# Attention products over 64 rows in pairs, and the float64 decode moved from attention to the experts

## Chip, core and metric

The kernel runs on one core of one Trainium2 chip. The metric is device time in microseconds (us) of one execution. Engines are TensorE (PE, with its weight loads listed as PEld), VectorE (DVE), ScalarE (ACT), GpSimd (POOL) and SyncE (SP), which issues transfers.

## The reference, cut to what matters

```
scores = (z @ z.T) / 3072            # 8 batches, 3072 x 64 each
x = u * (max(scores, 0)**2 @ v)      # v, u: 3072 x 256
e = argmax(x @ w_gate)               # 24576 tokens, 8 experts
x = gate * eom * (max(x @ w1[e], 0) @ w2[e])     # 256 -> 1024 -> 256
h = x @ w_in                         # w_in, w_out: float64
out = (h * sigmoid(h)) @ w_out       # 256 -> 2048 -> 256
```

All data but w_in and w_out are float32.

## The kernel before

There are three stages, one after the other. Every large product is made of rounded float32 numbers ("fp32r"): a float is split into a rounded part `hi` and a rest `lo`, and a product is the sum of hi*lo, lo*hi and hi*hi. `split` makes the two: the rounded copy on VectorE or ACT (L106, L108), the rest on VectorE (L109).

**Attention.** A chunk is 512 query columns; there are 48 chunks (6 for each of 8 batches), and each runs over 24 steps of 128 keys, 1152 steps in all. A step is `s_step` (scores, 2 products of 512 columns), `act_r` (relu on ACT), `act_a` (square on ACT), `dve_hl` (hi and lo on VectorE) and `v_step` (6 products of 512 columns that add up in two PSUM banks over the whole chunk, one for each half of v's 256 columns). As z has only 64 rows, `s_step` stacks z's hi and lo as one stationary tile `st` of 128 rows, made by `z_prep2` through two transfers on SP's queue, and multiplies it by z's hi and then z's lo, each of which stands twice, one below the other.

Program order is an order written out by hand: scores run 3 steps ahead of the sums (LOOK), and two tables of tasks (`pe_tasks` ahead of the step's sums, `tasks` behind) place the rest: loads, splits of v and z, the finished chunk's product with u (`x_mul`), its gate products (`gate_mm` at step 5, 4 products of 512 columns), `rank_mm` (step 10, 5 small products), page bookkeeping, `rep_mm` (step 14, 4 small ones) and the scatters of rows to `x_d` by POOL. [...]

`w_last` decodes the float64 weights of the last stage in 32 jobs of 256 columns: a load, 12 VectorE operations and one ACT copy, and a store of hi and lo to `wio_d`. The jobs run in attention, spread over the steps of a chunk.

**Experts.** 103 tiles of 256 tokens with 4 iterations each (412). An iteration is `s1` (12 products of 256 columns), a relu on ACT and a rest on VectorE, and `v1` (12 products of 256 columns), which runs two iterations behind `s1`. `w_split` splits the gathered weights (copy on ACT, rest on VectorE) four to six iterations ahead; `x1_prep` transposes and splits the next tile's tokens. ACT's queue reloads the decoded weights from `wio_d` in eight transfers.

**Last stage.** 768 iterations of 12 products of 512 columns, not touched by the change.

Of the kernel before, what the change touches and what calls it, by code (L numbers as in the profile page):

```python
# [30 lines left out]
P = 128  # L31
# [13 lines left out]
LOOK = 3  # L45
NEARLY = 20
# [6 lines left out]
def fused_kernel(ctx: ExitStack, tc: tile.TileContext, uT, v, zT, wg, w1, w2, w_in, w_out, out):  # L53
# [7 lines left out]
    wio_d = dram.tile([P, 2 * 2 * 2 * DFF], F32, name="wio_d")  # L61
# [3 lines left out]
    ps_s = ctx.enter_context(tc.tile_pool(name="ps_s", bufs=2, space=bass.MemoryType.PSUM))  # L65
    ps_a = ctx.enter_context(tc.tile_pool(name="ps_a", bufs=4, space=bass.MemoryType.PSUM))
    ps_m = ctx.enter_context(tc.tile_pool(name="ps_m", bufs=2, space=bass.MemoryType.PSUM))
# [110 lines left out]
    HH, LL, ST, ZZ, VH, VL, VR, UT = {}, {}, {}, {}, {}, {}, {}, {}  # L178
# [7 lines left out]
    def z_prep1(b, c):  # L186
        hh = zp.tile([P, CH], F32R, name="hh", tag="hh", bufs=6)
        ll = zp.tile([P, CH], F32R, name="ll", tag="ll", bufs=6)
        split(hh, ll, ZZ.pop((b, c)), "v" if b == 0 and c < 2 else "a")
        HH[b, c], LL[b, c] = hh, ll  # L190

    def z_prep2(b, c):
        st = zp.tile([P, CH], F32R, name="st", tag="st", bufs=9)
        if (b, c) == (0, 0):
            sc.activation(st[:DQK], HH[b, c][:DQK].bitcast(F32), AF.Copy)
            ve.tensor_copy(st[DQK:], LL[b, c][DQK:].bitcast(F32))
        else:
# [22 lines left out]
    wtmp = [small.tile([P, WJ], I32, name=f"wt{i}") for i in range(3)]  # L220
    NWJ = 2 * DFF // WJ

    def w_last(job):
        which, part = divmod(job, NWJ)
        src = (w_in, w_out)[which]
        raw = small.tile([P, WJ], I64, name="wraw", tag="wraw", bufs=1)
        sy.dma_start(raw, src[:, part * WJ:(part + 1) * WJ])
        words = raw.bitcast(I32).rearrange("p (n w) -> p n w", w=2)
        lw, hw = words[:, :, 0], words[:, :, 1]
        hi = small.tile([P, WJ], F32R, name="whi", tag="whi", bufs=1)  # L230
        lo = small.tile([P, WJ], F32R, name="wlo", tag="wlo", bufs=1)
        t, m, r = wtmp
        tf, mf, rf = (x.bitcast(F32) for x in wtmp)

        def store():
# [395 lines left out]
    for k in range(LOOK):  # L631
# [5 lines left out]
        if k < LOOK - 1:  # L637
            act_a(k)
            dve_hl(k)
# [405 lines left out]
```

## Time and profile before

| | |
|---|---|
| median of 3 runs | 5479.15 us (5478.13 to 5480.53) |
| the profiled execution | 5476.75 us, its span 5475.0 us |
| TensorE busy | 5449.3 us |
| VectorE, ACT, POOL busy | 4481.3, 2866.0, 2071.7 us |
| granted TensorE clock | 0.999 of full speed, mean |

The span runs from the first to the last instruction of the profiled execution. Busy time of an engine is the union of its instructions; consecutive matmuls overlap in it, so the distance of their starts says more than the length of one. Attention runs to about 2175 us, the experts to about 3380 us.

### The profile page before, as it was taken

To read this page: it belongs to the slowest core of one execution; us is meant where nothing else is said; L and a number is where in the kernel's file an instruction comes from. 1 tells how busy PE (TensorE), PEld (TensorE's weight loads), DVE (VectorE), ACT (ScalarE), POOL (GpSimd) and SP (SyncE) were. 2 spreads that over 40 slices of the span, in tenths; PEclk is the share of its full clock that TensorE was granted. 3 is DMA by queue.
4 is the path that set the end of the run, shared out by engine and by line. 5 is a ranking of instruction groups with operands and counts; after the bars stand their busy time and mean duration, and the time that the engine had idled before them with its cause. 6 is when DMAs were issued, how large, how long until landed. Compare 5 with 4: busy or idle time off the path is not lost.

```text
span 5475.0 us, 84633 instructions
## 1 busy us (share of the span) xinstructions
PE 5449.3 (100%) x28952; PEld 4690.0 (86%) x28952; DVE 4481.3 (82%) x9832; ACT 2866.0 (52%) x5076; POOL 2071.7 (38%) x1961
## 2 busy tenths in 40 slices
PE   9999999999999999999999999999999999999999
PEld 7888888888888887999999999888888888888887
DVE  8999999999999887878777777777777777777776
ACT  7777777777777766666666665222222222222222
POOL 0343333333333333443333335433333333333331
PEclk9999999999999999999999999999999999999999
DMA  8212121212122101244222221101000000100000
GB/s 281 63 54 63 51 62 51 62 53 60 55 58 55 50 24 53 80 146 164 93 78 78 78 78 37 26 24 28 24 24 25 24 24 24 28 24 24 25 24 21
DMA packets 160243, 314.99 MB, mean 58 GB/s; under 512 B 58560, under 2 KB 66752, under 8 KB 152384
## 3 DMA queue, kind: packets, MB, share of 16 engines
q0 software_dynamic: 95152, 156.97, 9.8%
q1 hardware_dynamic: 63504, 144.22, 8.3%
q10 hardware_dynamic: 1152, 8.39, 0.4%
q8 instruction: 226, 3.70, 0.3%
q14 instruction: 209, 1.71, 0.1%
HBM read 346.83 MB, written 112.72 MB: 84 GB/s over the span
## 4 chain that ended last, share of the span: by engine, by line
PE 96%; DVE 2%; issue 1%; DMA 0%; ACT 0%; POOL 0%; POOLq 0%; SPq 0%; DVEq 0%; ACTq 0%
PE s L854 19%; PE s L741 11%; PE acc L762 11%; PE acc L297 9%; PE acc L298 9%; PE acc L299 9%; PE acc L878 6%; PE acc L877 6%; PE acc L876 6%; PE sc L269 4%; PE sc L270 4%; PE lg L325 1%; DVE lo L109 0%; DVE hi L108 0%; DVE vl L109 0%
## 5 line engine op out<-in xcount | busy, mean ns | idle before, releaser
L466 POOL DMA_INDIRECT x_d<-z,xi x768 | 803.7, 1046 | 1422.0 <-DVE lo L109 812.2
L810 POOL DMA_INDIRECT yg<-y_d,yi x768 | 810.9, 1056 | 1216.0 <-DVE l L109 1106.1
L861 ACT ACTIVATE sg<-s 128x512 f32<-128x512 f32 x768 | 459.3, 598 | 1524.6 <-PE s L854 1342.0
L854 PE MATMUL s<-yh,wi 128*128 128x512 f32 x3072 | 1070.4, 389 | 0.1
L275 ACT ACTIVATE r<-sc 128x512 f32<-128x512 f32 x1152 | 688.6, 598 | 537.2 <-PE sc L270 512.5
L297 PE MATMUL acc<-hi,vl 128*128 128x512 f32 x2304 | 906.9, 394 | 0.0
L298 PE MATMUL acc<-lo,vh 128*128 128x512 f32 x2304 | 899.8, 391 | 1.4 <-DVE lo L109 1.4
L299 PE MATMUL acc<-hi,vh 128*128 128x512 f32 x2304 | 897.4, 389 | 0.0
L862 DVE TENSOR_TENSOR sg<-s,sg 128x512 f32<-128x512 f32 x768 | 531.2, 692 | 417.6 <-ACT sg L861 393.6
L109 DVE TENSOR_TENSOR lo<-a,hi 128x512 fp32r<-128x512 f32 x1152 | 798.9, 693 | 39.6
L280 ACT ACTIVATE a<-r 128x512 f32<-128x512 f32 x1152 | 726.4, 631 | 99.1 <-DVE lo L109 70.9
L854 PEld LDWEIGHTS s<-yh,wi 128*128 128x128 f32 x3072 | 576.6, 188 | 120.2 <-issue 0.5
L741 PE MATMUL s<-x1h,w0b 128*128 128x256 f32 x3296 | 662.9, 284 | 9.8 <-DVE w0b L109 9.7
L762 PE MATMUL acc<-w1b,h 128*128 128x256 f32 x3296 | 660.7, 283 | 0.0
L854 PE MATMUL s<-yl,wi 128*128 128x512 f32 x1536 | 597.7, 389 | 0.5 <-issue 0.5
L878 PE MATMUL acc<-h,wo 128*128 128x512 f32 x1536 | 597.5, 389 | 0.0
L877 PE MATMUL acc<-l,wo 128*128 128x512 f32 x1536 | 597.5, 389 | 0.0
L876 PE MATMUL acc<-h,wo 128*128 128x512 f32 x1536 | 597.5, 389 | 0.0
L108 DVE CAST hi<-a 128x512 fp32r<-128x512 f32 x1152 | 497.2, 432 | 87.4 <-ACT a L280 69.4
L741 PEld LDWEIGHTS s<-x1h,w0b 128*128 128x128 f32 x3296 | 545.0, 192 | 11.0 <-DVE w0b L109 9.3
L109 DVE TENSOR_TENSOR l<-sg,h 128x512 fp32r<-128x512 f32 x768 | 531.9, 693 | 26.5
L762 PEld LDWEIGHTS acc<-w1b,h 128*128 128x128 f32 x3296 | 543.7, 192 | 0.1
(200 smaller groups left out, 9655.0 us busy)
## 6 DMA issues: line engine op xcount, KB each, us to landing
x_d<-zero SPq DMA_DIRECT2D x25, 1024.0 KB
vr<-in_v_dram SPq DMA_DIRECT2D x48, 512.0 KB
ut<-in_uT_dram SPq DMA_DIRECT2D x48, 512.0 KB
out_dram<-ot SPq DMA_DIRECT2D x48, 512.0 KB
zz<-in_zT_dram SPq DMA_DIRECT2D x96, 128.0 KB
x_d<-z,xi POOLq DMA_INDIRECT x768
yg<-y_d,yi POOLq DMA_INDIRECT x768
st<-hh SPq DMA_DIRECT2D x47, 128.0 KB
```

The costliest lines, as they stand in the source:

```text
L109: return ve.tensor_sub(lo, src, hi.bitcast(F32))
L297: pe.matmul(ACC[q][dc], vl[:, j % 4, ds_], hi, start=(j == 0), stop=False)
L298: pe.matmul(ACC[q][dc], vh[:, j % 4, ds_], lo, start=False, stop=False)
L299: pe.matmul(ACC[q][dc], vh[:, j % 4, ds_], hi, start=False, stop=(j == NJ - 1))
L466: i = gp_.indirect_dma_start(x_u, bass.IndirectOffsetOnAxis(ap=xi4[:, q * NB + c:q * NB + c + 1], axis=0), Z[q][:, c, :], None, bounds_che ...
L741: pe.matmul(ps[:, i, :], wb[:, hl, dc, fs], xx[:, dc, :], start=(n == 0), stop=(n == 5))
L762: pe.matmul(acc[:, h, :], x[:, i, ts], wb[:, hl, i, :], start=first, stop=end, skip_group_check=True)
L810: i = gp_.indirect_dma_start(YG[m][:, c, :], None, y_u[:n, :], bass.IndirectOffsetOnAxis(ap=yi4[:, m * NB + c:m * NB + c + 1], axis=0), bo ...
L854: pe.matmul(ps, wi[:, hl, dc, fs], xx[:, dc, :], start=(n == 0), stop=(n == 5))
L876: pe.matmul(acc, wo[:, 1, fc, es], hi, start=(fc == 0), stop=False)
L877: pe.matmul(acc, wo[:, 0, fc, es], lo, start=False, stop=False)
L878: pe.matmul(acc, wo[:, 0, fc, es], hi, start=False, stop=(fc == FC2 - 1))
```

## The change

Scores are computed for two steps at once: `s_part` issues three products (hi*lo, lo*hi, hi*hi), each as two matmuls over 64 rows. The first uses rows 0 to 63 and belongs to the first step, the second uses rows 64 to 127 and belongs to the second step; they write two different banks. `v_part` issues each of the sums' products as two matmuls over 64 rows, too, each half with a PSUM bank of its own, so a chunk has four banks of sums. At the chunk's end `x_sum` copies one half from PSUM on ACT and adds the other on VectorE. The stationary tile `st` and its transfers are gone. Scores share four banks with the small products. Scores run six steps ahead. At four steps of a chunk the hi copy is made by ACT instead of VectorE. Some loads and splits of z are placed at other steps. The decode jobs run in the experts from iteration 96 on and write straight into the tiles that the last stage reads; `wio_d`, its stores and its reloads are gone, and the tables for the last stage are computed from iteration 73 on instead of 120. `x_gather` has three buffers instead of four, and the first `x1_prep` stands ahead of the fourth gather.

```diff
@@ -43,6 +43,9 @@
 HD = D // 4
 NFIRST = CH // T + E - 1
 LOOK = 3
+LA = 6
+ON_ACT = (7, 10, 11, 12)
+HP = P // 2
 NEARLY = 20
 QEARLY = NQ - 3
 WJ = 256
@@ -58,13 +61,11 @@
     dram = ctx.enter_context(tc.tile_pool(name="dram", bufs=1, space=bass.MemoryType.DRAM))
     x_d = dram.tile([NSLOT * P, 2 * T], F32, name="x_d")
     y_d = dram.tile([NSLOT * P, 2 * T], F32, name="y_d")
-    wio_d = dram.tile([P, 2 * 2 * 2 * DFF], F32, name="wio_d")
     x_u = x_d[:, :].rearrange("r (u c) -> (r u) c", c=HD)
     y_u = y_d[:, :].rearrange("r (u c) -> (r u) c", c=HD)
-    ps_s = ctx.enter_context(tc.tile_pool(name="ps_s", bufs=2, space=bass.MemoryType.PSUM))
+    ps_s = ctx.enter_context(tc.tile_pool(name="ps_s", bufs=4, space=bass.MemoryType.PSUM))
     ps_a = ctx.enter_context(tc.tile_pool(name="ps_a", bufs=4, space=bass.MemoryType.PSUM))
-    ps_m = ctx.enter_context(tc.tile_pool(name="ps_m", bufs=2, space=bass.MemoryType.PSUM))
     const = ctx.enter_context(tc.tile_pool(name="const", bufs=1))
     ident = const.tile([P, P], F32, name="ident")
@@ -184,20 +185,10 @@
         ZZ[b, c] = zz
     def z_prep1(b, c):
-        hh = zp.tile([P, CH], F32R, name="hh", tag="hh", bufs=6)
-        ll = zp.tile([P, CH], F32R, name="ll", tag="ll", bufs=6)
+        hh = zp.tile([P, CH], F32R, name="hh", tag="hh", bufs=9)
+        ll = zp.tile([P, CH], F32R, name="ll", tag="ll", bufs=9)
         split(hh, ll, ZZ.pop((b, c)), "v" if b == 0 and c < 2 else "a")
         HH[b, c], LL[b, c] = hh, ll
-
-    def z_prep2(b, c):
-        st = zp.tile([P, CH], F32R, name="st", tag="st", bufs=9)
-        if (b, c) == (0, 0):
-            sc.activation(st[:DQK], HH[b, c][:DQK].bitcast(F32), AF.Copy)
-            ve.tensor_copy(st[DQK:], LL[b, c][DQK:].bitcast(F32))
-        else:
-            sy.dma_start(st[:DQK].bitcast(F32), HH[b, c][:DQK].bitcast(F32))
-            sy.dma_start(st[DQK:].bitcast(F32), LL[b, c][DQK:].bitcast(F32))
-        ST[b, c] = st
     def v_load(b, g):
         vr = zp.tile([P, 4, D], F32, name="vr", tag="vr", bufs=2)
@@ -217,44 +208,6 @@
         UT[q] = ut
-    wtmp = [small.tile([P, WJ], I32, name=f"wt{i}") for i in range(3)]
-    NWJ = 2 * DFF // WJ
-
-    def w_last(job):
-        which, part = divmod(job, NWJ)
-        src = (w_in, w_out)[which]
-        raw = small.tile([P, WJ], I64, name="wraw", tag="wraw", bufs=1)
-        sy.dma_start(raw, src[:, part * WJ:(part + 1) * WJ])
-        words = raw.bitcast(I32).rearrange("p (n w) -> p n w", w=2)
-        lw, hw = words[:, :, 0], words[:, :, 1]
-        hi = small.tile([P, WJ], F32R, name="whi", tag="whi", bufs=1)
-        lo = small.tile([P, WJ], F32R, name="wlo", tag="wlo", bufs=1)
-        t, m, r = wtmp
-        tf, mf, rf = (x.bitcast(F32) for x in wtmp)
-
-        def store():
-            for h, x in ((0, hi), (1, lo)):
-                o = (which * 2 + h) * 2 * DFF + part * WJ
-                sy.dma_start(wio_d[:, o:o + WJ], x.bitcast(F32))
-
-        return [
-            lambda: ve.tensor_scalar(t, lw, 29, 7, ALU.logical_shift_right, ALU.bitwise_and),
...
-            store,
-        ]
-
-
     SC, RR, AA, HI, LO, ACC = {}, {}, {}, {}, {}, {}
     def bcj(k):
@@ -262,17 +215,34 @@
         b, c = divmod(q, NCH)
         return q, b, c, j
-    def s_step(k):
-        q, b, c, j = bcj(k)
-        ps = ps_s.tile([P, CH], F32, name="sc", tag="sc")
-        lhs = ST[b, j // 4][:, (j % 4) * P:(j % 4 + 1) * P]
-        pe.matmul(ps, lhs, HH[b, c], start=True, stop=False)
-        pe.matmul(ps, lhs, LL[b, c], start=False, stop=True)
-        SC[k] = ps
+
+
+    def halves(x, y, a, b, start, stop):
+        return [
+            pe.matmul(out, x[h][h * HP:(h + 1) * HP, w], y[h][h * HP:(h + 1) * HP, m], start=start, stop=stop,
+                      skip_group_check=True)
+            for h, (w, m, out) in enumerate((a, b))
+        ]
+
+    def s_part(k, parts):
+
+        for i in range(2):
+            if k + i not in SC:
+                SC[k + i] = ps_s.tile([P, CH], F32, name="sc", tag="sc")
+        at_ = []
+        for i in range(2):
+            q, b, c, j = bcj(k + i)
+            at_.append((b, c, j // 4, slice(j % 4 * P, (j % 4 + 1) * P), SC[k + i]))
+        for n in parts:
+            wx, mx = ((HH, LL), (LL, HH), (HH, HH))[n]
+            halves(
+                [wx[b, g] for b, c, g, js, ps in at_], [mx[b, c] for b, c, g, js, ps in at_],
+                *[(js, slice(0, CH), ps) for b, c, g, js, ps in at_], n == 0, n == 2,
+            )
     def act_r(k):
-        r = ap_.tile([P, CH], F32, name="r", tag="r", bufs=2)
-        sc.activation(r, SC.pop(k), AF.Relu, scale=1.0 / S)
+        r = ap_.tile([P, CH], F32, name="r", tag="r", bufs=3)
+        sc.activation(r, SC[k], AF.Relu, scale=1.0 / S)
         RR[k] = r
     def act_a(k):
@@ -281,32 +251,40 @@
         AA[k] = a
     def dve_hl(k):
-        hi = ap_.tile([P, CH], F32R, name="hi", tag="hi", bufs=4)
-        lo = ap_.tile([P, CH], F32R, name="lo", tag="lo", bufs=4)
-        beat.append(split(hi, lo, AA.pop(k)))
+        hi = ap_.tile([P, CH], F32R, name="hi", tag="hi", bufs=6)
+        lo = ap_.tile([P, CH], F32R, name="lo", tag="lo", bufs=6)
+        beat.append(split(hi, lo, AA.pop(k), "a" if k % NJ in ON_ACT else "v"))
         HI[k], LO[k] = hi, lo
-    def v_step(k):
+    def v_part(k, d):
+
         q, b, c, j = bcj(k)
-        if j == 0:
-            ACC[q] = [ps_a.tile([P, CH], F32, name=f"acc{d}", tag="acc") for d in range(2)]
-        hi, lo = HI.pop(k), LO.pop(k)
-        vh, vl = VH[b, j // 4], VL[b, j // 4]
-        for dc in range(2):
-            ds_ = slice(dc * P, (dc + 1) * P)
-            pe.matmul(ACC[q][dc], vl[:, j % 4, ds_], hi, start=(j == 0), stop=False)
-            pe.matmul(ACC[q][dc], vh[:, j % 4, ds_], lo, start=False, stop=False)
-            pe.matmul(ACC[q][dc], vh[:, j % 4, ds_], hi, start=False, stop=(j == NJ - 1))
+        if q not in ACC:
+            ACC[q] = [[ps_a.tile([P, CH], F32, name=f"acc{i}{h}", tag="acc") for h in range(2)] for i in range(2)]
+        hi, lo = HI[k], LO[k]
+        vh, vl = VH[b, j // 4][:, j % 4, :], VL[b, j // 4][:, j % 4, :]
+        ds_ = slice(d * P, (d + 1) * P)
+        for n, (v, x) in enumerate(((vl, hi), (vh, lo), (vh, hi))):
+            halves([v, v], [x, x], *[(ds_, slice(0, CH), ACC[q][d][h]) for h in range(2)],
+                   j == 0 and n == 0, j == NJ - 1 and n == 2)
     XH, XL, Z, G = {}, {}, {}, {}
-    def x_mul(q, dc):
+    def x_sum(q, dc):
         if dc == 0:
             XH[q] = xp.tile([P, 2, CH], F32R, name="xh", tag="xh", bufs=1)
             XL[q] = xp.tile([P, 2, CH], F32R, name="xl", tag="xl", bufs=1)
             Z[q] = xp.tile([P, NB, HD], F32, name="z", tag="z", bufs=3)
-        ve.tensor_mul(UT[q][:, dc, :], ACC[q][dc], UT[q][:, dc, :])
+        n = NB // 2
+        t = Z[q][:, dc * n:(dc + 1) * n, :].rearrange("p n c -> p (n c)")
+        sc.activation(t, ACC[q][dc][1], AF.Copy)
+        ve.tensor_add(t, ACC[q][dc][0], t)
+
+    def x_mul(q, dc):
+        n = NB // 2
+        t = Z[q][:, dc * n:(dc + 1) * n, :].rearrange("p n c -> p (n c)")
+        ve.tensor_mul(UT[q][:, dc, :], t, UT[q][:, dc, :])
     def x_hi(q, dc):
         sc.activation(XH[q][:, dc, :], UT[q][:, dc, :], AF.Copy)
@@ -318,7 +296,7 @@
         ve.transpose(Z[q][:, :, dc * Q:(dc + 1) * Q], UT[q][:, dc, :])
     def gate_mm(q):
-        ps = ps_m.tile([P, CH], F32, name="lg", tag="misc")
+        ps = ps_s.tile([P, CH], F32, name="lg", tag="sc")
         n = 0
         for dc in range(2):
             for xx in (XL[q], XH[q]):
...
@@ -567,9 +545,7 @@
         last = first + (NCH - 1) * NJ
         for c in range(NCH):
             at(first + c * NJ + 12, z_load, b, c)
-            at(first + c * NJ + 26, z_prep1, b, c)
-            at(first + c * NJ + 28 if c < 3 else last + 4 * (c - 3) + 4 if c < NCH - 1 else last + 28,
-               z_prep2, b, c)
+            at(first + c * NJ + 20 if c < 3 else last + (4, 8, 20)[c - 3], z_prep1, b, c)
             s1_ = first + (c + 1) * NJ + 16 if c < 3 else last + (6, 15, 17)[c - 3]
             at(s1_ - 6, v_load, b, c)
             at(s1_, v_prep, b, c, 0)
@@ -598,29 +574,21 @@
                 left.append((q, [c]))
     for s, f in ((13, order1), (16, order1_mm), (16, order2), (19, order2_mm), (19, order3)):
         at((QEARLY + 1) * NJ + s, f, 0, pe=f in ON_PE)
-    WSTEPS = (8, 9, 13, 15, 16, 17, 18, 19, 21, 21, 22, 22, 23, 23)
-    for job, q in zip(range(2 * NWJ), [q for q in range(1, NQ) if q % NCH < NCH - 1]):
-        k = q * NJ
-        at(k + 2, lambda k=k, job=job: [at(k + i, f) for i, f in zip(WSTEPS, w_last(job))])
-
     z_load(0, 0)
     v_load(0, 0)
     z_load(0, 1)
     z_prep1(0, 0)
-    z_prep2(0, 0)
     z_load(0, 2)
     v_load(0, 1)
     z_prep1(0, 1)
-    z_prep2(0, 1)
     at(0, v_load, 0, 2)
     at(0, z_prep1, 0, 2)
-    at(0, z_prep2, 0, 2)
     at(3, u_load, 0)
     at(3, lambda: sy.dma_start(wgr, wg))
     for c in range(3, NCH):
-        at(4 * c - 9, lambda c=c: (z_load(0, c), v_load(0, c)))
-        at(4 * c - 7, z_prep1, 0, c)
-        at(4 * c - 6, z_prep2, 0, c)
+        at(4 * c - 12, z_load, 0, c)
+        at(4 * c - 9, v_load, 0, c)
+        at(4 * c - 9, z_prep1, 0, c)
     for c in range(1, NCH):
         at(max(4 * c - 4, 0), v_prep, 0, c, 0)
         at(4 * c - 3, v_prep, 0, c, 1)
@@ -628,27 +596,38 @@
     for i in range(0, NSLOT, 4):
         at(5 + i if i < 12 else 11 + i // 2, zero_pages, i, 4)
     at(6, gate_matrix)
-    for k in range(LOOK):
-        s_step(k)
+    for k in range(LA):
+        if k % 2 == 0:
+            s_part(k, (0, 1, 2))
         act_r(k)
         if k == 0:
             v_prep(0, 0, 0)
             v_prep(0, 0, 1)
-        if k < LOOK - 1:
+        if k < LA - 2:
             act_a(k)
             dve_hl(k)
     for k in range(NSTEP):
-        if k + LOOK < NSTEP:
-            s_step(k + LOOK)
         for f, a in pe_tasks.pop(k, []):
             f(*a)
-        v_step(k)
-        if k + LOOK - 1 < NSTEP:
-            act_a(k + LOOK - 1)
-        if k + LOOK < NSTEP:
-            act_r(k + LOOK)
-        if k + LOOK - 1 < NSTEP:
-            dve_hl(k + LOOK - 1)
+        q, j = divmod(k, NJ)
+
+        if k % 2 == 0:
+            v_part(k, 0)
+            v_part(k + 1, 0)
+            if k + LA < NSTEP:
+                s_part(k + LA, (0, 1, 2))
+            v_part(k, 1)
+            v_part(k + 1, 1)
+        elif k - 1 + LA < NSTEP:
+            act_r(k - 1 + LA)
+            act_r(k + LA)
+        if j == NJ - 1:
+            x_sum(q, 1)
+        if k + LA - 2 < NSTEP:
+            act_a(k + LA - 2)
+            dve_hl(k + LA - 2)
+        if j == NJ - 2:
+            x_sum(q, 0)
         for f, a in tasks.pop(k, []):
             f(*a)
     assert not tasks and not pe_tasks
@@ -701,7 +680,7 @@
     def x_gather(t):
         if t >= NSLOT:
             return
-        xg = wp.tile([P, 2 * T], F32, name="xg", tag="xg", bufs=4)
+        xg = wp.tile([P, 2 * T], F32, name="xg", tag="xg", bufs=3)
         g = gp_.indirect_dma_start(
             xg, None, x_d[:, :], bass.IndirectOffsetOnAxis(ap=table(xidx, t), axis=0),
             bounds_check=NSLOT * P - 1, oob_is_err=False,
@@ -771,12 +750,37 @@
             yt.rearrange("p h d -> p (h d)"), None, bounds_check=NSLOT * P - 1, oob_is_err=False,
         )
-    def w_load(dst, o, i):
-        n = 4 * DFF // 4
-        sc.dma_start(
-            dst.rearrange("p a b c -> p (a b c)")[:, i * n:(i + 1) * n].bitcast(F32),
-            wio_d[:, o + i * n:o + (i + 1) * n],
-        )
+
+    NWJ = 2 * DFF // WJ
+
+    def w_last(job):
+        which, part = divmod(job, NWJ)
+        w = (wi, wo)[which].rearrange("p a b c -> p a (b c)")[:, :, part * WJ:(part + 1) * WJ]
+        hi, lo = w[:, 0, :], w[:, 1, :]
+        raw = mp.tile([P, WJ], I64, name="wraw", tag="wraw", bufs=1)
+        words = raw.bitcast(I32).rearrange("p (n w) -> p n w", w=2)
+        lw, hw = words[:, :, 0], words[:, :, 1]
+        wt = mp.tile([P, 3, WJ], I32, name="wt", tag="ya", bufs=1)
+        t, m, r = (wt[:, i, :] for i in range(3))
+        tf, mf, rf = (x.bitcast(F32) for x in (t, m, r))
+        return [
+            lambda: sy.dma_start(raw, (w_in, w_out)[which][:, part * WJ:(part + 1) * WJ]),
+            lambda: None,
+            lambda: None,
...
+            lambda: sc.activation(hi, tf, AF.Copy),
+            lambda: ve.tensor_sub(tf, tf, hi.bitcast(F32)),
+            lambda: ve.tensor_add(lo, tf, rf),
+        ]
     def y_index():
@@ -924,8 +928,8 @@
     x_gather(2)
     w_gather(1, 0)
     w_gather(1, 1)
+    x1_prep(0)
     x_gather(3)
-    x1_prep(0)
     w_split(0, 0)
     w_split(1, 0)
     w_split(0, 1)
@@ -960,10 +964,19 @@
         for f, a in late.get(k, []):
             if f not in ON_PE:
                 f(*a)
-        if k == 120:
+        if k == 73:
             yops = y_index()
-        if k > 120 and yops:
+        if k > 73 and yops:
             yops.pop(0)()
+        if k >= 96:
+            if k == 96:
+                jobs = list(range(2 * NWJ))
+                nd = 16 * len(jobs)
+                dops, dn = [], 0
+            while (dops or jobs) and dn * 296 < nd * (k - 95):
+                dops = dops or w_last(jobs.pop(0))
+                dops.pop(0)()
+                dn += 1
         if k == 72:
             xs.close()
             wr = moe.enter_context(tc.tile_pool(name="wr", bufs=1, side="right", reuse_waits="tile"))
@@ -975,9 +988,7 @@
             YL[0] = wr.tile([P, 2, CH], F32R, name="yl0")
             wr.tile([P, 8], F32, name="wr_gap")
-        if k in range(80, 160, 10):
-            w_load(*((wi, 0), (wo, 4 * DFF))[k >= 120], k // 10 % 4)
-    assert not yops
+    assert not yops and not dops and not jobs
     p1.close()
     lp = moe.enter_context(tc.tile_pool(name="lp", bufs=2, reuse_waits="tile"))
```

## Rows read from the trace of the kernel before

**Rows 1.** The page: the span, and each engine's busy time.

```profile
span 5475.0 us, 84633 instructions
PE 5449.3 (100%) x28952; PEld 4690.0 (86%) x28952; DVE 4481.3 (82%) x9832; ACT 2866.0 (52%) x5076; POOL 2071.7 (38%) x1961
```

**Rows 2.** Busy time by stretch: attention, experts, experts; the header names the columns.

```profile
core 0: us, PE busy (x) PEld busy (x) DVE busy (x) ACT busy (x) POOL busy (x), PEclk, DMA share, GB/s
...
1000.00:1500.00 500.00, 499.61 (x2274) 408.43 (x2273) 465.76 (x1337) 352.28 (x621) 186.42 (x178) 1.00 0.20 57
2500.00:2900.00 400.00, 399.87 (x3332) 399.62 (x3331) 311.05 (x508) 261.58 (x486) 152.27 (x140) 1.00 0.29 93
2900.00:3300.00 400.00, 400.00 (x3336) 400.00 (x3335) 302.75 (x487) 262.56 (x486) 152.88 (x140) 1.00 0.25 79
```

**Rows 3.** Timeline of TensorE in attention: start us, us, engine, line, operation.

```profile
1000.82 0.39 PE L269 MATMUL sc<-hh,st 128*128 128x512 f32 x1
1001.05 0.39 PE L270 MATMUL sc<-ll,st 128*128 128x512 f32 x1
...
1002.63 0.39 PE L269 MATMUL sc<-hh,st 128*128 128x512 f32 x1
```

**Rows 4.** Timeline of TensorE in the experts, twelve products apart.

```profile
2701.49 0.28 PE L741 MATMUL s<-x1h,w0b 128*128 128x256 f32 x1
2701.49 0.19 PEld L741 LDWEIGHTS s<-x1l,w0b 128*128 128x128 f32 x1
...
2702.93 0.28 PE L762 MATMUL acc<-w1b,h 128*128 128x256 f32 x1
```

**Rows 5.** Timeline of TensorE at one chunk's rank products.

```profile
2151.74 0.19 PE L370 MATMUL rk<-oh,upper 128*128 128x32 bf16 x1
...
2151.78 0.24 PE L372 MATMUL rk<-oh,ones_b 128*128 128x32 bf16 x4
...
2151.88 0.47 PE L297 MATMUL acc<-hi,vl 128*128 128x512 f32 x1
```

**Rows 6.** Waits of TensorE in the whole span: us in total, times, longest.

```profile
PE s L741 <- DVE w0b L109: 9.7, 2, 8.9
PE sc L269 <- DVE st L196: 6.0, 1, 6.0
PE sc L269 <- DMA st<-ll: 1.6, 1, 1.6
```

**Rows 7.** Groups of instructions, 1000 to 1500 us: busy us, mean ns, idle before.

```profile
L109 DVE TENSOR_TENSOR lo<-a,hi 128x512 fp32r<-128x512 f32 x267 | 185.2, 694 | 9.2
L280 ACT ACTIVATE a<-r 128x512 f32<-128x512 f32 x267 | 168.3, 630 | 24.0 <-DVE lo L109 17.5 <-DVE isn L414 0.9
L275 ACT ACTIVATE r<-sc 128x512 f32<-128x512 f32 x267 | 159.6, 598 | 121.9 <-PE sc L270 118.7 <-PE acc L299 2.1 <-issue 0.8
L108 DVE CAST hi<-a 128x512 fp32r<-128x512 f32 x266 | 114.6, 431 | 13.7 <-ACT a L280 9.1 <-issue 0.8 <-ACT r L275 0.7
...
L309 DVE TENSOR_TENSOR ut<-acc,ut 128x512 f32<-128x512 f32 x22 | 15.0, 684 | 0.0
```

**Rows 8.** The same view: first and last of the decode's twelve VectorE groups.

```profile
L250 DVE SCALAR_TENSOR_TENSOR wt<-wt,wt 128x256 f32<-128x256 int32 x10 | 4.5, 454 | 0.3
...
L246 DVE TENSOR_SCALAR wt<-wt 128x256 int32<-128x256 int32 x9 | 2.6, 287 | 0.0
```

**Rows 9.** Timeline of TensorE: first gate product, and the product after the four.

```profile
2141.70 0.40 PE L325 MATMUL lg<-xl,gm 128*128 128x512 f32 x1
...
2142.63 0.40 PE L297 MATMUL acc<-hi,vl 128*128 128x512 f32 x1
```

**Rows 10.** Groups of instructions in the experts, 2500 to 3300 us: next tile's tokens.

```profile
L723 DVE STREAM_TRANSPOSE xt<-xg 128x512 f32<-128x512 f32 x69 | 48.4, 702 | 0.0
L109 DVE TENSOR_TENSOR x1l<-xt,x1h 128x512 fp32r<-128x512 f32 x69 | 47.8, 693 | 48.1 <-ACT x1h L106 48.1
```

**Rows 11.** Timeline of TensorE: a product whose weights were not loaded ahead.

```profile
3321.37 0.39 PE L741 MATMUL s<-x1h,w0b 128*128 128x256 f32 x1
...
3321.59 0.28 PE L741 MATMUL s<-x1l,w0b 128*128 128x256 f32 x1
```

More of the change, by code (lines that the diff above doesn't have):

```diff
@@ L176, in gate_matrix @@
             ve.tensor_copy(gm[:, :, i * Q:(i + 1) * Q], gm[:, :, 0:Q].bitcast(F32))
-    HH, LL, ST, ZZ, VH, VL, VR, UT = {}, {}, {}, {}, {}, {}, {}, {}
+    HH, LL, ZZ, VH, VL, VR, UT = {}, {}, {}, {}, {}, {}, {}
     def z_load(b, c):
@@ L367, in rank_mm @@
     def rank_mm(q):
-        ps = ps_m.tile([P, 5, E], F32, name="rk", tag="misc")
+        ps = ps_s.tile([P, 5, E], F32, name="rk", tag="sc")
         oh = G[q, "oh"]
@@ L445, in rep_mm @@
     def rep_mm(q):
-        ps = ps_m.tile([P, 4, 2, 4], F32, name="rp", tag="misc")
+        ps = ps_s.tile([P, 4, 2, 4], F32, name="rp", tag="sc")
         pb = G.pop((q, "pb"))
@@ L522, in order1_mm @@
     def order1_mm(i):
-        ps = ps_m.tile([P, P], F32, name="ok", tag="misc")
+        ps = ps_s.tile([P, P], F32, name="ok", tag="sc")
         pe.matmul(ps, ones_f, TB[i][2], start=True, stop=True)
@@ L542, in order2_mm @@
         oneh, erow = TB[i]
-        ps = ps_m.tile([P, 2, P], F32, name="pt", tag="misc")
+        ps = ps_s.tile([P, 2, P], F32, name="pt", tag="sc")
         pe.matmul(ps[:, 0, :], prow, oneh, start=True, stop=False, skip_group_check=True)
@@ L772, in y_store @@
         )
-    def w_load(dst, o, i):
-        n = 4 * DFF // 4
-        sc.dma_start(
-            dst.rearrange("p a b c -> p (a b c)")[:, i * n:(i + 1) * n].bitcast(F32),
-            wio_d[:, o + i * n:o + (i + 1) * n],
-        )
+    NWJ = 2 * DFF // WJ
[13 more added lines that the diff above has]
+            lambda: None,
+            lambda: ve.tensor_scalar(t, lw, 29, 7, ALU.logical_shift_right, ALU.bitwise_and),
+            lambda: ve.scalar_tensor_tensor(t, hw, 3, t, ALU.logical_shift_left, ALU.bitwise_or),
+            lambda: ve.tensor_scalar(t, t, 0x7FFFFFFF, 0x40000000, ALU.bitwise_and, ALU.bitwise_xor),
+            lambda: ve.scalar_tensor_tensor(t, hw, -0x80000000, t, ALU.bitwise_and, ALU.bitwise_or),
+            lambda: ve.tensor_scalar(m, hw, 20, 0x7FF, ALU.logical_shift_right, ALU.bitwise_and),
+            lambda: ve.tensor_scalar(m, m, 897, -1, ALU.is_ge, ALU.mult),
+            lambda: ve.tensor_tensor(t, t, m, ALU.bitwise_and),
+            lambda: ve.tensor_scalar(m, t, -0x800000, None, ALU.bitwise_and),
+            lambda: ve.tensor_scalar(r, lw, 0x1FFFFFFF, None, ALU.bitwise_and),
+            lambda: ve.scalar_tensor_tensor(rf, r, 2.0**-52, mf, ALU.mult, ALU.mult),
+            lambda: sc.activation(hi, tf, AF.Copy),
+            lambda: ve.tensor_sub(tf, tf, hi.bitcast(F32)),
+            lambda: ve.tensor_add(lo, tf, rf),
+        ]
     def y_index():
```

12 lines of the change are left out of this document (removed).

## The prediction

> **What bounds the kernel now.** I read the engine shares first, then busy times by stage, then single products on TensorE, then who waits for whom. The shares say that TensorE is busy for 5449.3 of 5475.0 us [rows 1]. The stages say that this holds inside attention and inside the experts alike: 499.61 of 500 us in attention, 399.87 and 400.00 of 400 us in the experts [rows 2]. VectorE is next, with 465.76 of 500 us (93%) in attention and 77% in the experts (613.8 of 800) [rows 2]; at 93% it did not hold TensorE up. All waits of TensorE over 1 us are three: 9.7 us between attention and the experts, 6.0 us at the very start, 1.6 us for a copied stationary tile in the start-up [rows 6]. So time comes from the number of products and the distance between their starts.
>
> That distance is the figure on which all rests. One attention step is eight products, and the first product of one step starts 1.81 us after that of the step before (1000.82 to 1002.63) [rows 3], so 0.2266 us for 512 columns. In the experts twelve products of 256 columns take 1.44 us, 0.120 us each [rows 4]. The difference of 256 columns costs 0.1066 us, so a product is 0.2133 us (or 0.1067 us) of columns and 0.0133 us of something else. The recorded 0.39 us of one product is longer than the distance, as products overlap at their ends.
>
> An attention chunk (24 steps) issues 192 such products, four gate products, five rank products and four index products, 205 in all; 2274 products in 500 us are 11.09 chunks, so a chunk takes 45.1 us [rows 2].
>
> **The change, part by part.** *Scores and sums.* A pair of steps had 4 full score products and 12 full sum products, 16 distances. Afterwards it has 3 score products and 12 sum products, each as two halves of 64 rows, 15 pairs of halves. If the halves of a pair run side by side, a pair of halves takes what one full product took, 0.2266 us. A step then costs 7.5 distances instead of 8: 1152 steps x 0.5 x 0.2266 = 130.5 us less. No row shows a product over 64 rows. From below, a pair can't beat its columns alone: 0.2133 us. From above, two halves one after the other are 0.453 us. Between them lies the weights' bound: each half brings its own 128-column weights, and the shortest distance at which the trace shows such fp32 weights loaded is 0.120 us [rows 4]; if the two loads of a pair can't overlap, the pair takes up to 0.240 us. I take 0.2266 us: in the experts the distance follows the columns to the same 0.0133 us remainder, so the rows do not show that the load was what set it there. Issue itself isn't near: five small products with five weight loads start within 0.14 us (2151.74 to 2151.88), 0.028 us each [rows 5], against four instructions in 0.2266 us.
>
> [...]
>
> *Changes of shape.* The gate, rank and index products stay over 128 rows, at three places in a chunk, so the array changes between 64 and 128 rows six times a chunk, 288 times in all. The trace before has no such change. From below it costs nothing. From above it costs the end of the running product, 0.39 - 0.2266 = 0.163 us, and weights that could not be loaded ahead: where that happens (3321.37) the next product follows after 0.22 us instead of 0.12 us, 0.10 us more [rows 11]; together 0.263 us. I take the end alone, 0.163 us, because the product after the rank group starts right behind it although the shape of the data changed [rows 5]: 288 x 0.163 = 46.9 us (0 to 75.7).
>
> [...]
>
> *Four accumulators at the chunk's end.* Before, two banks of four were in use, and the next chunk had the other two. Now all four are one chunk's, so the first sum product of the next chunk waits until the last chunk's two banks are read: an ACT copy of 0.598 us (priced by the row of the relu, which also reads 128x512 from PSUM) and a VectorE add of 0.684 us (the row of the multiply that reads an accumulator) [rows 7]. In the last pair of a chunk the products run in the order sums of the first half of v's columns (6 pairs, 1.36 us), scores (0.68 us), sums of the second (1.36 us). The first accumulators are ready at 1.36 + 0.16 = 1.52 us; the copy ends at about 2.2 us. The add stands behind the step's own hi and lo on VectorE (0.431 + 0.694 us, twice in the pair); their input comes from two relus and two squares on ACT (0.598 and 0.630 us) after the scores of the pair before, so they end at about 2.9 us, and the add at 3.6 to 3.7 us. The next chunk's first sum is due at 3.40 us: a wait of 0.3 us. The second accumulators have 3.4 + 2.04 us until they are due and are read by 4.9 us. What is queued behind the waiting product is the next scores; they are six steps ahead, so nobody waits for them. 48 x 0.3 = 14.4 us; below 0, above, with one more hi and lo in front of the add, 48 x 1.4 = 68 us.
>
> *VectorE and ACT in attention.* The decode leaves: twelve VectorE operations a job whose means add up to 4.37 us (from 0.454 us down to 0.287 us) [rows 8]. About 9.5 jobs fall into the 500 us, 3.7 us of a chunk's 42.0 us. Four hi copies a chunk go to ACT (4 x 0.431 us less), two adds come (2 x 0.684 us more): 37.9 us of a chunk of about 43.7 us, 87%. ACT has 31.8 us a chunk now [rows 2], and gains four hi copies at about 0.63 us and two of 0.598 us: 35 us, 80%. Both are below the 93% that TensorE did not feel, so nothing is charged; without that cover each step lost would be up to 0.1 us. Gate products (0.93 us for four, 2141.70 to 2142.63 [rows 9]) are unchanged; they now use the score banks, four instead of two, and their readers are one pair ahead of need.
>
> *Decode in the experts.* 32 jobs x 4.37 us = 140 us of VectorE fall into 296 iterations of 24 products, 2.88 us each, 852 us: 16% on top of 77%, so 93% again. A weak place is the transposition of the next tile: VectorE waits 48.1 us for 69 tiles, 0.70 us each, inside it [rows 10], idle time that it can't fill; with it the load is 99%. The wait would reach TensorE's first product of a tile. Lower bound 0; upper bound, half a microsecond for each of the 74 tiles, 37 us; I take 5 us, as lo and the weight splits run two iterations and more ahead. SP's queue has little else in this stage, and a decode job's load is issued about 1.7 iterations (5 us) before its first reader. The eight 1 MB reloads by ACT's queue and the stores go; nothing waited for them.
>
> *Start-up.* The stationary copy and its transfers go: the 1.6 us wait [rows 6] goes with them. The last expert stage is untouched.
>
> Sum against the profiled execution, 5476.75 us (2.4 us under the median of the runs): -130.5 + 46.9 + 14.4 + 5 - 1.6 = -65.8, which gives **5411 us**.
>
> **Rivals.** *The weights bind* (slower). A pair at 0.240 us costs 8640 pairs x 0.0134 = 116 us more: 5527 us. For it: in the experts the weight loads cover all 400 us and leave no gap [rows 2], and a pair needs two. Against it: the remainder of 0.0133 us at both widths [rows 3, 4]. It decides from a pair of 0.2266 + 65.8/8640 = 0.234 us on.
>
> *The halves don't overlap at all.* Then a pair is 0.453 us and the kernel takes 5411 + 8640 x 0.2266 = 7369 us. Nothing in the trace excludes it, as every product there uses 128 rows.
>
> *The remainder goes too* (much faster). If one half's fixed 0.0133 us lies beside the other half's columns, a pair is 0.2133 us: 115 us less, 5296 us. A chunk would be about 41.3 us with 37.9 us of VectorE, 92%, still possible.
>
> **How the numbers follow.** I give my forecast 0.52, the weights' bound 0.24, the lost remainder 0.13, no overlap 0.07, and 0.04 to small mishaps that end just above the time before. The forecast's own range, from no cost for changes of shape to their full cost with a longer wait at the chunk's end, is 5345 to 5480 us. The range that holds all but two in ten goes from the lost remainder (5300) to a little over the weights' bound (5540). About 0.2% (11 us) is what a measurement of this kernel can tell from no change. Faster: 0.49 of my forecast, 0.13, and 0.01 of the weights' bound with free shape changes, 0.63. Same: 0.03 and 0.03, 0.06. Slower: 0.20, 0.07 and 0.04, 0.31.
>
> **What would show it.** Starts of the same half of successive pairs in attention: 0.2266 us apart if I am right, 0.240 us if weights bind. The two halves of a pair start almost together if they overlap. Around the gate products, gaps of about 0.16 us at each edge. At a chunk's end, TensorE waits for the VectorE add, about 0.3 us. In the experts, VectorE at 93% and TensorE without waits. I am wrong if the distance of pairs is over 0.234 us, or if waits for VectorE or ACT appear inside chunks.

## The result, and the profile after

The changed kernel takes 5425.15 us (median of 4 runs, 5424.41 to 5427.09), beside 5478.64 us for the kernel before: ratio 0.9903, 95% interval 0.9891 to 0.9915. The forecast was 5411 us, with a range of 5300 to 5540 us. Measured again beside the experiments it took 5416.09 us (ratio 0.9894, 0.9877 to 0.9910) and 5425.27 us (0.9906, 0.9890 to 0.9921), so its time differs by about 9 us from one occasion to the next, and the intervals of the ratio overlap. Most of the 9 us lies in attention: the experts' first product starts at 2120.97 us in the shorter occasion and at 2128.23 us in the profiled execution below.

The page of the profiled execution after, against [rows 1]: span and busy times.

```profile
span 5422.9 us, 101815 instructions
PE 5375.3 (99%) x37016; PEld 4645.0 (86%) x37016; DVE 4439.2 (82%) x9735; ACT 2903.5 (54%) x5363; POOL 2068.7 (38%) x1961
```

8064 more products and weight loads are issued (37016 against 28952), and TensorE is busy for 74 us less. The halves of a pair lie over each other. The timeline of TensorE after, one pair of steps, against [rows 3] (`x2` are two products in a row of one kind, here the two halves; as the row is no longer than one product, 0.39 us, both start within 0.01 us):

```profile
1000.12 0.39 PE L222 MATMUL acc<-hi,vh 64*128 64x512 f32 x2
...
1001.48 0.39 PE L222 MATMUL acc<-hi,vh 64*128 64x512 f32 x2
1001.71 0.39 PE L222 MATMUL sc<-ll,hh 64*128 64x512 f32 x2
...
1003.52 0.39 PE L222 MATMUL acc<-hi,vh 64*128 64x512 f32 x2
```

From 1000.12 to 1003.52 are the fifteen pairs of two steps in 3.40 us, 0.2267 us each: a pair of halves takes what one full product took.

Busy time by stretch after, against [rows 2]: attention, and twice the experts while the decode runs there.

```profile
1000.00:1500.00 500.00, 494.27 (x4253) 409.24 (x4251) 440.39 (x1260) 368.78 (x693) 188.61 (x182) 1.00 0.14 42
2500.00:2900.00 400.00, 399.75 (x3313) 398.03 (x3312) 351.67 (x664) 263.42 (x499) 153.00 (x137) 1.00 0.27 85
2900.00:3300.00 400.00, 399.57 (x3307) 397.45 (x3306) 347.66 (x651) 262.40 (x496) 170.89 (x151) 1.00 0.26 82
```

A chunk now has 373 products (360 halves and the 13 small and gate ones), so 4253 of them are 11.40 chunks and a chunk takes 43.9 us instead of 45.1. TensorE idles 5.7 of 500 us in attention, which it did not before. In the experts VectorE rose from 77% to 87%, not to the 93% of the forecast: the 29 decode jobs in these 800 us have 125 us of instructions and added 85.5 us of busy time, in part because instructions in a row overlap at their ends (a decode row of 0.29 us starts at 2703.29 and the next at 2703.49). TensorE stays busy there, but it issues 3313 and 3307 products where it issued 3332 and 3336: their starts lie a little further apart.

The waits of TensorE in the whole span after, against [rows 6] (us in total, times, longest):

```profile
PE s L720 <- issue: 10.3, 2, 10.1
PE rp L427 <- DVE pb L399: 9.5, 24, 1.3
PE sc L222 <- DVE ll L110: 5.7, 1, 5.7
PE acc L222 <- DVE z L282: 5.6, 12, 1.0
PE acc L222 <- ACT z L281: 2.4, 1, 2.4
PE ok L502 <- DVE dk L497: 1.4, 1, 1.4
```

The first is the change to the experts, the third the start; both were there before. New are the waits of the index products for VectorE, which I did not foresee, and the two for `x_sum` at the chunk's end, which I did. This view counts only time in which TensorE is idle. A product's row lasts 0.39 us where the next one starts after 0.227 us, so up to 0.16 us of each late start doesn't show in it; and if only one half of a pair is late, the other half keeps TensorE busy and the wait doesn't show at all (the pair of 1021.40 below is one row of 0.85 us). What the waits cost is taken from starts below.

### The profile page after: what moved, and what is told of

Read it like the earlier page. It is cut to its first block, busy times and chain, and to the rows that moved or that the text cites. A ratio compares the mean times of both kernels' runs of the same rounds, so it can differ in the third digit from the quotient of the medians.

```text
span 5422.9 us, 101815 instructions
## 1 busy us (share of the span) xinstructions
PE 5375.3 (99%) x37016; PEld 4645.0 (86%) x37016; DVE 4439.2 (82%) x9735; ACT 2903.5 (54%) x5363; POOL 2068.7 (38%) x1961
## 5 line engine op out<-in xcount | busy, mean ns | idle before, releaser
L222 PE MATMUL acc<-hi,vl 64*128 64x512 f32 x4608 | 1018.9, 395 | 8.4 <-DVE z L282 5.6
L222 PE MATMUL acc<-lo,vh 64*128 64x512 f32 x4608 | 1000.6, 387 | 0.3 <-DVE lo L110 0.2
L222 PE MATMUL acc<-hi,vh 64*128 64x512 f32 x4608 | 998.1, 387 | 0.0
L245 ACT ACTIVATE r<-sc 128x512 f32<-128x512 f32 x1152 | 623.0, 593 | 365.1 <-PE sc L222 309.7
L250 ACT ACTIVATE a<-r 128x512 f32<-128x512 f32 x1152 | 703.3, 630 | 112.8 <-DVE lo L110 108.3
L222 PEld LDWEIGHTS acc<-hi,vl 64*128 64x128 f32 x4608 | 523.0, 184 | 108.6 <-issue 17.1
L222 PEld LDWEIGHTS acc<-hi,vh 64*128 64x128 f32 x4608 | 521.6, 184 | 76.2
L222 PEld LDWEIGHTS acc<-lo,vh 64*128 64x128 f32 x4608 | 519.6, 184 | 70.8 <-DVE lo L110 1.3
```

Of the source, the lines that this page charges most:

```text
L222: pe.matmul(out, x[h][h * HP:(h + 1) * HP, w], y[h][h * HP:(h + 1) * HP, m], start=start, stop=stop, skip_group_check=True)
L245: sc.activation(r, SC[k], AF.Relu, scale=1.0 / S)
L250: sc.activation(a, RR.pop(k), AF.Square)
```

## Experiments

Each changes the kernel after unless it says otherwise. Experiments 1, 2, 3 and 10 are single runs; the others have an interval. The kernel after was not measured beside 1 to 4, so a difference from it is good to about 10 us there.

**1. Do the weight loads of a pair run side by side?** The scores' pairs run over 256 columns twice.

```diff
-            halves(..., *[(js, slice(0, CH), ps) ...], n == 0, n == 2)
+            for m in (slice(0, CH // 2), slice(CH // 2, CH)):
+                halves(..., *[(js, m, ps[:, m]) ...], n == 0, n == 2)
```

> The scores' pairs of halves run over 256 columns twice instead of 512 once; all else stays. If the weight loads of the two halves of a pair run beside each other, pairs of 256 columns start 0.120 us apart, as single products of 256 columns do in the experts: the scores of a pair of steps take 0.72 us instead of 0.68 us, and the kernel about 23 us more, 5448 us. If the two loads follow one another (0.107 to 0.120 us each) and are only hidden by 512 columns, such pairs start 0.213 to 0.240 us apart: the scores take 1.28 to 1.44 us, and the kernel 340 to 440 us more.

5438.64 us, 13 to 23 us more than the kernel after, as the first branch had it. The timeline of TensorE in this kernel (`x4`: two pairs of 256 columns):

```profile
1001.98 0.40 PE L222 MATMUL sc<-ll,hh 64*128 64x256 f32 x4
1002.21 0.40 PE L222 MATMUL sc<-hh,ll 64*128 64x256 f32 x4
...
1002.69 0.40 PE L222 MATMUL acc<-hi,vl 64*128 64x512 f32 x2
```

From 1002.21 to 1002.69 are four pairs in 0.48 us, so a pair of 256 columns with its two weight loads takes 0.120 us, the time that one product of 256 columns with one load takes [rows 4]. Two loads one after the other would have taken 0.213 to 0.240 us by the expectation. Loads of the two row groups (rows 0 to 63, rows 64 to 127) therefore ran side by side here, and the rival "the weights bind" is out.

**2 and 10. Must the halves alternate?** In the sums all products of the upper rows are issued ahead of those of the lower rows, three in a row, and in a second kernel six in a row (both steps of a pair).

```diff
-        for n, (v, x) in enumerate(...):
-            halves([v, v], [x, x], ...)
+        for h in range(2):
+            for n, (v, x) in enumerate(...):
+                pe.matmul(ACC[q][d][h], v[r_, ds_], x[r_, :], ...)   # r_: 64 rows of half h
```

> In the sums the three products of the upper 64 rows are issued first, then the three of the lower 64 rows, instead of in turn. If products start in program order, only the last of one row group overlaps the first of the other: six halves take four distances instead of three, 16 a pair of steps instead of 12, and the kernel takes 576 x 4 x 0.2266 = 522 us more, about 5950 us. If TensorE picks products of the free row group ahead of waiting ones, nothing changes, 5425 us.

> In the sums, six products of the upper 64 rows (two steps) are issued in a row, then the six of the lower 64 rows. With three in a row the halves still ran side by side, their starts 10 ns apart. If each row group runs its own list of products as long as issue is ahead, the starts lie 20 ns apart and the time stays at that of the changed kernel, 5416 to 5425 us. If the look ahead is shorter than six products, some halves run alone: for one of six 0.2266 x 2 x 576 = 261 us more, and so on.

Three in a row: 5415.77 us, no loss, where 522 us was expected. The timeline of that kernel still shows the first product of both halves starting together and then the second of both, although the program has all three of one half first:

```profile
1001.31 0.40 PE L270 MATMUL acc<-hi,vl 64*128 64x512 f32 x2
1001.54 0.40 PE L270 MATMUL acc<-lo,vh 64*128 64x512 f32 x2
1001.77 0.40 PE L270 MATMUL acc<-hi,vh 64*128 64x512 f32 x2
```

Six in a row: 5493.46 us, 68 us more than the kernel after beside it (5425.27 us). Its timeline behind a chunk's rank products shows one row group fall behind the other:

```profile
1255.55 0.49 PE L284 MATMUL acc<-hi,vl 64*128 64x512 f32 x1
...
1256.11 0.39 PE L284 MATMUL acc<-hi,vh 64*128 64x512 f32 x1
1256.12 0.62 PE L284 MATMUL acc<-hi,vl 64*128 64x512 f32 x2
...
1256.92 0.39 PE L284 MATMUL acc<-hi,vl 64*128 64x512 f32 x1
1257.03 0.39 PE L222 MATMUL sc<-ll,hh 64*128 64x512 f32 x1
```

The lower rows' first product (in the `x2` row of 1256.12) starts only with the third of the upper rows (1256.11), 0.57 us late; three of the upper rows' products are then still ahead of it in program order. From there one row group is on its scores while the other is still on the sums ahead of them. So products in different row groups were not held to program order in these two runs: a product came past two and past three waiting ones of the other group, and in the rows above not past four. I read the 68 us as this lag, lost at the next product over 128 rows, three times in a chunk; by my estimate that is 0.47 us each time (68 us over 144).

**3. What does a change between 64 and 128 rows cost?** The sums go back to 128 rows and one bank, so `x_sum` only copies and adds nothing; the scores stay paired.

```diff
-            halves([v, v], [x, x], ...)
+            pe.matmul(ACC[q][d], v[:, ds_], x, ...)
```

> The sums go back to 128 rows and one bank each (no adding of halves at the chunk's end); the scores stay in 64-row pairs. If each change between 64 and 128 rows costs about 0.2 us of TensorE, two changes in each of 576 pairs of steps cost 240 us, while those around the gate, rank and index products (60 us) and the waits for the halves' sum (8 us) go: about 5425 + 175 = 5600 us. If a change of shape is free and the gaps at the gate products have another cause, the kernel takes 5425 - 8 us or less.

5597.56 us, as expected of the first theory. The timeline of TensorE in this kernel around one set of scores:

```profile
1000.71 0.39 PE L268 MATMUL acc<-hi,vh 128*128 128x512 f32 x1
1001.03 0.50 PE L222 MATMUL sc<-ll,hh 64*128 64x512 f32 x2
1001.36 0.40 PE L222 MATMUL sc<-hh,ll 64*128 64x512 f32 x2
1001.60 0.39 PE L222 MATMUL sc<-hh 64*128 64x512 f32 x2
1001.92 0.50 PE L268 MATMUL acc<-hi,vl 128*128 128x512 f32 x1
1002.25 0.40 PE L268 MATMUL acc<-lo,vh 128*128 128x512 f32 x1
```

At each change the first product comes 0.32 us after the last instead of 0.227, and the second 0.33 us after the first: 0.09 + 0.10 = 0.2 us. This is why the sums, which gain nothing by halving, must be halved with the scores.

**4. One more pair of changes in a chunk.** The four gate products are issued as two at step 4 and two at step 6.

```diff
-(5, gate_mm)
+(4, gate_half, 0), (6, gate_half, 1)
```

> The four gate products of a chunk are issued as two and two, a pair of steps apart, so that a chunk has eight changes of shape instead of six; the amount of work stays. If a change costs about 0.2 us, 48 x 2 x 0.21 = 20 us more than 5425 us. If the gaps at the gate products are a wait for the score bank that they now share, the second two products meet a bank already theirs, and the time stays within 5 us of 5425 us.

5466.34 us (ratio 0.9981, 0.9972 to 0.9991), twice the expected loss. The waits of TensorE in this kernel say why:

```profile
PE lg L302 <- DVE xl L293: 26.8, 46, 0.8
```

The earlier step made the first two products wait for their operand: 26.8 us of the 41 to 50 us (against 5425.15 and 5416.09 us) are that, not the changes. The second two did not wait, and their rows give the price of one more pair of changes:

```profile
1008.47 0.41 PE L222 MATMUL acc<-hi,vh 64*128 64x512 f32 x2
1008.81 0.50 PE L302 MATMUL lg<-xl,gm 128*128 128x512 f32 x1
...
1009.48 0.50 PE L222 MATMUL acc<-hi,vl 64*128 64x512 f32 x2
1009.82 0.39 PE L222 MATMUL acc<-lo,vh 64*128 64x512 f32 x2
```

From the sum ahead of the two gate products to the second sum behind them are 1.35 us where four distances are 0.91 us: 0.44 us there (0.42 us on the mean of the chunks), 0.2 us for each change and 20 us in all, as expected.

**5 and 6. The decode's place.** The kernel before with the decode alone moved to the experts (with the changed `x_gather` buffers and the earlier tables that go with it); and the kernel after with the decode, its stores and its reloads back in attention (jobs from the fifth chunk on, in buffers that other tiles use too).

```diff
-    at(k + 2, lambda k=k, job=job: [at(k + i, f) for i, f in zip(WSTEPS, w_last(job))])
+        if k >= 96: ...   # w_last(job) in the experts' loop, as in the change
```

> The kernel before with the decode alone moved to the experts. If VectorE at 93% held nothing up in attention and the experts take the 140 us of decode at a price of 5 us, the kernel takes about 5 us more than before, 5484 us. If the decode did cost attention time, it takes less than before; if the decode saturates VectorE in the experts, up to 37 us more.

> The changed kernel with the decode back in attention (its tiles reuse the buffer of zeros, and the jobs start at the fifth chunk). VectorE then has about 41.5 us in a chunk of 43.4 us, 96%, with waits for ACT on top. If that is too much at the shorter chunk, TensorE waits about half a microsecond more in each chunk with a job: 32 x 0.5 = 16 us, less the 5 us in the experts: about 5436 us. If VectorE still hides it, the 5 us in the experts come back: 5420 us.

Alone: 5479.22 us (ratio 1.0008, 0.9998 to 1.0017), no change that can be measured; in its trace the experts take 4.4 us more than before (1196.28 against 1191.83 us). Back in attention: 5462.21 us (ratio 0.9976, 0.9966 to 0.9985), 46 us more than the kernel after, measured beside it; the expectation had 11 us more or 5 us less than 5425 us. TensorE's waits there:

```profile
PE acc L260 <- DVE z L320: 32.5, 40, 1.5
PE rp L465 <- DVE pb L437: 24.8, 41, 1.3
```

They were 4.0 and 6.9 us in the kernel after beside it, 46.4 us less. The experts' first product starts 52.9 us later (2173.91 against 2120.97 us) and the experts are 5.0 us shorter, so these waits are most of the loss. VectorE was busy for 455.31 of 500 us in this kernel, 91%, less than the 93% that TensorE hardly felt before. The move gives nothing by itself; with the shorter chunk it is worth 46 us.

**7, 9, 11. Fewer changes, and the waits.** The index products move beside the next chunk's gate products (7); the bookkeeping behind them is spread too (9); the last nine chunks keep the old places and the scatters start earlier (11).

```diff
-        (14, rep_mm), (14, x_index), (15, gate_s)
+        r_ = (q + 2) * NJ + 5            # 7: beside gate_mm of the next chunk
+        s = {pages2: 13, pages3: 16, gate_s: 19}.get(f, s)   # 9
+        k = max(..., 70 + 6 * (q * NB + c) // 5)             # 11: 70 was 76
```

> The changed kernel with the index products of a chunk moved beside the gate products of the next one (15 steps later, all but the last three chunks), and its scatters 15 steps later. Two changes of shape a chunk go (2 x 0.21 us), and the wait for the index products' operand (9.5 us in all): 44 x 0.42 + 9.5 = 28 us less than 5425 us, 5397 us. If the gap is not tied to the shape but to the place at the start of a pair, only the 9.5 us go: 5416 us.

> The index products stay beside the next chunk's gate products, and the bookkeeping that no longer has a product waiting for it moves out of the dense half of the chunk: pages2 from step 11 to 13, pages3 from 12 to 16, gate_s from 12 to 19. If the 0.68 us that TensorE waited at about step 16 of a chunk with the index products joined is VectorE's backlog, it goes in 44 chunks: 25 to 30 us less than with them joined, about 5398 us where the changed kernel takes 5416 us. If the wait belongs to the hi and lo of that step themselves, the time stays at 5427 us.

> As the spread version, but the last nine chunks keep the old places, so that scatters and index products do not pile up at the end of attention (the last chunks and the change to the experts took some 16 us more there), and the scatters start six steps earlier, so that the fourth chunk's first sum does not wait for the first chunk's scatters (2.4 us, and about as much again at the lower clock). If both are the causes, 39 chunks gain about 0.17 us each and the fourth chunk some 4 us: about 10 us less than the changed kernel, a ratio to the kernel before of 0.988 to 0.989. If the waits only move once more, the ratio stays at 0.990 to 0.991.

5426.98 us (ratio 0.9912, 0.9895 to 0.9928) for 7, 5432.32 us (0.9919, 0.9905 to 0.9932) for 9, 5422.80 us (0.9903, 0.9886 to 0.9919) for 11. None of the three gains came: no version beats the kernel after. For 11 the other branch of its expectation holds (the ratio stays, the waits move); 7 and 9 came out above both of theirs, 7 at 11 us and 9 at 7 us more than the kernel after beside them (the intervals of the ratios overlap). With 7, TensorE waited for `lo` instead (43 times, 9.5 us idle). TensorE's waits with the spread version:

```profile
PE acc L222 <- DVE z L282: 17.4, 29, 1.6
PE s L725 <- DVE w0b L110: 14.8, 2, 14.1
```

The waits for the index products' operand are gone. They came back as waits for the add at the chunk's end (17.4 us against 6.5 us in the kernel after beside it) and at the change to the experts. With 11, the fourth chunk's wait for ACT went (a later chunk, at 1847 us, has one of 1.9 us), and the waits for the add stayed at 15.5 us. I read this as VectorE's order of work setting what is left beside the changes of shape. That is an argument from where the waits went; no run here takes VectorE's work away.

**The kernel after beside these** was run twice:

> The changed kernel itself, beside the others on the same chip: 5425 us.

> The changed kernel itself, beside the others on the same chip: 5416 to 5425 us.

Both results stand at the head of the section on the result.

## Why the prediction was right

**Products.** Both sides of the main term held: 7.5 distances a step, 0.2267 us each, 130.5 us. That the halves run side by side was an assumption, which no row of before showed; after, both start within 0.01 us. The value between the bounds (0.2133 to 0.453 us) was right because each row group loads its own weights beside the other, which run 1 showed (a pair of 256 columns every 0.120 us); the argument I gave for it, the same 0.0133 us at both widths, was no proof. The rivals without overlap (0.453 us), and with the remainder lost (0.2133 us), fell with the 0.2267 us.

**Changes of shape.** Forecast 46.9 us, between 0 and 75.7. A change between full products cost 0.2 us (run 3): about half is a gap (0.09 us), and half lies on the second product behind the change (0.10 us). The timeline of TensorE after at one chunk's rank products, against [rows 5]:

```profile
1040.03 0.39 PE L222 MATMUL acc<-hi,vh 64*128 64x512 f32 x2
1040.36 0.19 PE L348 MATMUL rk<-oh,upper 128*128 128x32 bf16 x1
...
1040.57 0.50 PE L222 MATMUL acc<-hi,vl 64*128 64x512 f32 x2
1040.90 0.39 PE L222 MATMUL acc<-lo,vh 64*128 64x512 f32 x2
```

And the same place in the kernel before, around the lines of [rows 5]:

```profile
2151.51 0.39 PE L270 MATMUL sc<-ll,st 128*128 128x512 f32 x1
...
2152.19 0.40 PE L298 MATMUL acc<-lo,vh 128*128 128x512 f32 x1
```

From the last product ahead of the rank products to the second behind them it is 0.87 us after and 0.68 us before. The late second product (0.33 us after, 0.31 us before) is no cost of the change here: it was there without one. So the rank products' two changes cost 0.19 us, and the index products' the same on the mean of the chunks. The gate products, which take full width, cost the 0.4 us of run 3 (0.37 us on the mean). A chunk loses 0.75 us, 36 us in all, 11 us less than the forecast. I charged the end of the running product at every change and no weights that come late. That a change costs this whole end, 0.163 us, was my estimate, and no run shows it: at each edge the gap is 0.09 to 0.10 us, and the small products cost half as much as the gate's.

**The chunk's end.** Forecast 14.4 us (48 waits of 0.3). The view of waits has only 13 waits and 8.0 us, because most of it doesn't show as idle time. The timeline of VectorE and TensorE after, at a chunk's end and at its gate products ten us later:

```profile
1021.01 0.68 DVE L282 TENSOR_TENSOR z<-acc,z 128x512 f32<-128x512 f32 x1
1021.17 0.39 PE L222 MATMUL acc<-hi,vh 64*128 64x512 f32 x2
1021.40 0.85 PE L222 MATMUL acc<-hi,vl 64*128 64x512 f32 x2
...
1031.66 0.61 PE L222 MATMUL acc<-hi,vh 64*128 64x512 f32 x2
1032.20 0.50 PE L303 MATMUL lg<-xl,gm 128*128 128x512 f32 x1
```

One half of the next chunk's first sum starts on time, the other after the VectorE add, which ends at 1021.69 us (the row of both is 0.85 us instead of 0.39). One row group then stays behind by 0.22 us (rows of 0.61 us) until the gate products, which use all rows: they start 0.54 us after the last pair, where most rank products of this trace start after 0.32 us. By the starts of all products, such lags and the delays at the chunk's end come to 21 us more than before over the chunks, 4.8 us of them in the fourth. Its cause I missed: `x_sum` writes `z` at the chunk's end, six steps ahead of where `x_tr` wrote it, and the fourth chunk's `z` is the first chunk's buffer, which POOL's scatters to `x_d` still read. The waits of ACT there:

```profile
ACT z L281 <- DMA x_d<-z,xi: 4.3, 1, 4.3
```

The granted clock fell behind it, as the windows of that place show (the two numbers after the busy times' last bracket are clock and DMA share):

```profile
182.00:185.00 3.00, 1.09 (x10) 0.56 (x6) 0.28 (x1) 0.19 (x1) 0.97 (x1) 1.00 0.04 11
185.00:188.00 3.00, 2.31 (x11) 1.67 (x13) 1.75 (x4) 2.90 (x6) 0.00 (x0) 0.76 0.01 3
188.00:191.00 3.00, 3.00 (x20) 2.36 (x20) 2.29 (x4) 1.25 (x3) 1.76 (x2) 0.67 0.04 11
```

TensorE idled 1.9 of 3 us, and in the 6 us behind that its granted clock was 0.76 and then 0.67 of full speed on the mean.

**VectorE in attention.** Here a step failed: "nothing is charged". The prediction itself named waits for VectorE inside chunks as a sign of being wrong, and they came: at 88% VectorE left the index products late in nearly every chunk, as the chunk's tasks crowd its first two thirds. An example behind the last line of the first timeline above:

```profile
1004.06 0.25 PE L427 MATMUL rp<-pb,rep 128*128 128x8 bf16 x4
```

They start 0.54 us after the sum of 1003.52, where 0.32 us is the distance without a wait (that of most rank products in this trace). By starts this is 15.6 us in all, and 1.6 us more at the rank products, where the view of waits has 9.5 us. The 93% before was no proof of cover, and it was not quite free either (TensorE waited for `lo` seven times, 1.4 us): 93% hid nearly all there, and 88% here and 91% in run 6 (46 us) did not. I read this as a matter of how long TensorE can go on without the late result.

**Experts.** Forecast 5 us. From the first product of the experts to the first of the last stage it was 1191.83 us before (2184.88 to 3376.71) and is 1197.16 us after (2128.23 to 3325.39): 5.3 us. Run 5 has 4.4 us for the decode's move alone.

**The sum.** From the starts of products: -130.5 + 36 (shape) + 21 (chunk's end) + 17 (late index and rank products) + 1.4 (the order products' wait) - 2.7 (start-up) + 5.3 (experts) + 1.2 (the change to the experts, 10.5 against 9.3 us) - 0.9 (last stage) = -52.2 us; the spans differ by 52.1 us. So the mechanism and the main term were right, and the closeness of 5411 to 5425 us is in part luck: shape was charged 11 us too much, the chunk's end and VectorE together 24 us too little.

## What to carry to other kernels

Products that use half of the array's rows are worth pairing when the pair removes a product, and then everything around them should use the same shape, as each change there and back cost 0.4 us between full products and 0.19 us around the small ones here (with the sums over 128 rows the kernel took 5597.56 us). When TensorE gets faster, look again at every engine that was "hidden": at 91% VectorE cost 46 us here, where 93% had cost almost nothing at the longer chunk (1.4 us of waits for `lo`). Take the price of a late product from the distances of starts, as idle time shows only part of it (9.5 of 15.6 us for the index products). Moving a wait's cause isn't removing it: three versions that took waits from one place found them at the next.

## What the runs showed of the hardware that I had not expected

Products in different row groups ran out of program order in runs 2 and 10. With three products of one group issued ahead of three of the other, the halves still started together; with six, one group fell behind the other and the kernel took 68 us more (5493.46 against 5425.27 us).

Weight loads of two row groups took no more time than one in run 1: two loads of 128 fp32 columns and two products of 256 columns over 64 rows started every 0.120 us, as one load and one full product of 256 columns do in the kernel before (0.120 us, [rows 4]).

In the kernel after, two row groups ran 0.22 us apart for ten us at no cost that the starts show: in this stretch fifteen pairs took 3.40 us (1027.12 to 1030.52), as without the lag (1000.12 to 1003.52). It was paid at the next product over 128 rows (0.54 us behind the last pair, 1031.66 to 1032.20, instead of 0.32 us).
